# Reordering one stretch of a fused attention and highway kernel: batch 2's query exps and sums around batch 1's x

## The chip, the core and the metric

The kernel runs on one core of one Trainium2 chip. A core has five engines with queues of their own: TensorE (PE, matrix products), VectorE (DVE), ScalarE (ACT), GpSimd (POOL) and SyncE (SP, which here issues the transfers). PE writes its products into PSUM, which holds eight banks; the other operands lie in SBUF. The metric is the device time of a run in microseconds (us), as the median over several runs.

## The reference

Two layers follow each other. The first is a linear attention without a square score matrix: the queries are softmaxed over their 64 features, the keys over the 576 tokens, and a 64 by 64 product of keys and values is applied to the queries. The second is a highway layer over the joined heads.

```python
q_s = exp(q - max(q, -1));  q_s = q_s / (sum(q_s, -1) + 1e-09)
k_s = exp(k - max(k, 2));   k_s = k_s / (sum(k_s, 2) + 1e-09)
kv  = einsum('bhsd,bhse->bhde', k_s, v)
x   = einsum('bhsd,bhde->bhse', q_s, kv)      # then (4608, 512), heads side by side
H   = maximum(x @ w_h, 0)
T   = 1 / (1 + exp(-(x @ w_t + b_t)))
out = T * H + (1 - T) * x
```

There are 8 batches, 8 heads, 576 tokens and 64 features; inputs and output are 32-bit.

## The kernel before, in words

**Attention, one batch at a time.** `load` brings q, k and v of a batch (1152 KB each) into SBUF over SP's queue, in the order in which the loads are written. `exp_half` lets ACT take the exp of half the heads of q or k into a 16-bit tile (eq, ek). The query sums are either one DVE reduction per half (`q_sums`) or, for batches 1 and 2, a tree of two halving adds and a short reduction (`q_sums_tree`, L228 to L230); `q_recip` inverts them on DVE, and `q_scale_p` multiplies eq by them on POOL in pieces of tokens. `cast_v` and `cast_v_head` bring v to 16 bits, on POOL or ACT, with a column of ones behind every head, so that one product gives both the key-value product and the key sums. `q_trans` turns eq on PE (tile pq, three groups of tokens) and copies it to qsT on DVE. `kv_half` accumulates the key-value products of two heads' pairs in psk (two banks, called for half 0 and half 1), and `kv_norm` divides by the key sums on DVE (rz, kvn). `x_pair` multiplies qsT by kvn into two banks (px) for the first 512 tokens and copies each to the 16-bit tile xT, one on ACT and one on DVE; `x_left` does the last 64 tokens of all heads in two small products (px_l), copied by DVE to x9.

**Highway layer, one chunk at a time.** Chunk c is the first 512 tokens of batch c; chunks 8 and 9 gather all batches' last tokens. For each of four blocks of 128 output features, `gate` does four products into a bank pt, and ACT takes the tanh of it in place; `carry` does four products into a bank ph, and DVE makes relu(ph) minus x in one operation, the difference dd (L332); `blend` is a second DVE operation, (tanh + 1) times dd, into the 16-bit tile g (L340). `out_tile` turns x + g/2 back on PE (bank nat), copies it to 32 bits and stores it.

**PSUM.** Three pools share the eight banks: `ps_ht` has four (pt and ph), `ps_q` three (pq, psk, px, px_l) and `ps_nat` one. A new tile takes the bank that was freed first; PE waits until the last reader of that bank is done.

**Order.** Nothing is scheduled by a planner: the order of the Python calls is the order on every queue. First a list is run from top to bottom (the start, batches 0 and 1, chunk 0). After it come the entries of `events`, sorted by their place; chunk c lies at 8c to 8c + 7, with its gate of block ob at 8c + 2ob, its carry one later and its blend two later. The preparation of batch b is placed between the products of chunk b - 1, from the table with the places of its transposes (tr), key-value halves (kv) and x products (x). Within one place the order of insertion counts. Each engine works through its queue in that order, and an instruction that has to wait holds up all behind it on its engine.

Of the kernel before, what the change touches and what calls it, by code (L numbers as in the profile page):

```python
# [9 lines left out]
FP32 = mybir.dt.float32  # L10
# [8 lines left out]
def kernel(  # L19
# [10 lines left out]
    nc = tc.nc  # L30
    B, H, S, D = q.shape
    P = 128
    PAD = 128
    N9 = S // 64
    NM = N9 - 1
# [20 lines left out]
    ps_ht = pool("ps_ht", 4, space=PSUM)  # L56
    ps_q = pool("ps_q", 3, space=PSUM)
# [205 lines left out]
        else:  # L263
            nc.vector.tensor_copy(qsT[b][:, :, n0:n1, :], t[:, :, 0:w, :])  # L264

    def x_pair(b, a, even=False):
        g, b2 = b // 2, b % 2
        if a == 0 and b2 == 0:
            xT[g] = xtp.tile([P, 4, NM, 2, 64], FP16, tag="xT", name=f"xT_{g}")
        t = [  # L270
            ps_q.tile([P, NM, 64], FP32, tag="qx", name=f"px_{b}_{a}_{c}")
            for c in range(2)
        ]
        for x in range(2):
            for c in range(2):
                r = slice(64 * c, 64 * c + 64)
                mm(
                    t[c][64 * x : 64 * x + 64].rearrange("p n d -> p (n d)"),
                    kvn[b % 2][r, x, a, :],
                    qsT[b][r, 2 * a + x, 0:NM, :].rearrange("p n d -> p (n d)"),  # L280
                    True, True,
                )
        for c in range(2):
            dst = xT[g][:, 2 * a + c, :, b2, :]
            if (c == 0) if even else (a + c < 2):
                nc.scalar.copy(dst, t[c])  # L286
            else:
                nc.vector.tensor_copy(dst, t[c])  # L288
# [17 lines left out]
    def views(c):  # L306
        if c >= B:
            h = slice(4 * (c - B), 4 * (c - B) + 4)
            return lambda k_: x9[:, k_, h], lambda k_: g9[:, k_, h]
        g, b2 = c // 2, c % 2  # L310
        if g not in gT:
            gT[g] = gp.tile([P, 4, NM, 2, 64], FP16, tag="g", name=f"g_{g}")
        return lambda k_: xT[g][:, k_, :, b2, :], lambda k_: gT[g][:, k_, :, b2, :]

    live = {}
# [8 lines left out]
        live[c, ob] = ps  # L324

    def carry(c, ob):
        xv = views(c)[0]
        ps = ps_ht.tile([P, rows_of(c), 64], FP32, tag="ht", name=f"ph_{c}_{ob}")
        for k_ in range(4):
            mm(ps, w16["h"][:, k_, ob * P : ob * P + P], xv(k_), k_ == 0, k_ == 3)  # L330
        dd = mo.tile([P, rows_of(c), 64], FP16, tag="dd", name=f"dd_{c}_{ob}")
        nc.vector.scalar_tensor_tensor(  # L332
            dd, ps, 0.0, xv(ob), op0=ALU.max, op1=ALU.subtract
        )
        live[c, ob] = (live[c, ob], dd)
# [76 lines left out]
    def at(p, *fs):  # L412
        events.setdefault(p, []).extend(fs)

    E = lambda f, *a: (lambda: f(*a))

    for c in range(1, B + 2):
        for ob in range(4):
            p = 8 * c + 2 * ob
            at(p, E(gate, c, ob))  # L420
            at(p + 1, E(carry, c, ob))
# [14 lines left out]
    at(p + 4, E(tile9, 1, 4))  # L436
    at(p + 8, E(tile9, 2, 3), E(tile9, 3, 3), E(last9))

    at(8, E(exp_half, 2, "q", 1), E(cast_v, 2, 0))
    at(9, E(cast_v_head, 2, 2, nc.gpsimd))  # L440
    at(10, E(exp_half, 2, "k", 0), E(q_sums_tree, 2, 1), E(q_recip, 2))
    at(10, E(q_scale_p, 2, 0, 4), E(q_scale_p, 2, 4, 8), E(q_scale_p, 2, 8, N9))
    at(11, E(cast_v_head, 2, 3, nc.scalar), E(exp_half, 2, "k", 1))
    for b in range(2, B):
        p = 8 * (b - 1)
        if b > 2:
            s = p + {3: -2, 4: -4}.get(b, -5)
            at(s, E(exp_half, b, "q", 0))
            at(s + 1, E(exp_half, b, "q", 1), E(q_sums, b, 0))
            at(s + 2, E(q_sums, b, 1), E(q_recip, b))  # L450
            if b > 3:
                at(s + 2, E(q_scale_p, b, 0, 4))
                at(s + 3, E(q_scale_p, b, 4, N9))
            s = p + {3: 0, 4: 0}.get(b, -1)
            at(s, E(exp_half, b, "k", 0), E(cast_v, b, 0))
            at(s + 1, E(exp_half, b, "k", 1), E(cast_v, b, 1))
            if b == 3:
                at(p + 1, E(q_scale_p, b, 0, 4), E(q_scale_p, b, 4, N9))
        tr, kv, x = {
            2: ((5, 6, 6), (4, 5), (6.5, 7.5, 7.5)),  # L460
            3: ((4, 5, 5), (3, 4), (6, 7, 7)),
            4: ((2, 3, 4), (4, 5), (6, 6, 7)),
        }.get(b, ((2, 3, 4), (3, 4), (5, 6, 7)))
        for i in range(3):
            at(p + tr[i], E(q_trans, b, i))
        at(p + kv[0], E(kv_half, b, 0))
        at(p + kv[1], E(kv_half, b, 1), E(kv_norm, b))
        at(p + x[0], E(x_pair, b, 0))
        at(p + x[1], E(x_pair, b, 1))
        at(p + x[2], E(x_left, b))  # L470
# [3 lines left out]
    for f in [  # L474
        E(warm_up, 20),
        E(exp_half, 0, "q", 0), E(q_sums, 0, 0),
        E(exp_half, 0, "q", 1), E(q_sums, 0, 1),
        E(q_recip, 0), E(q_scale_v, 0, 0, 4), E(q_scale_v, 0, 4, N9),
        E(exp_half, 0, "k", 0), E(cast_v, 0, 0),
        E(exp_half, 0, "k", 1), E(cast_v, 0, 1),  # L480
        E(q_trans, 0, 0), E(q_trans, 0, 1), E(warm_up, 2), E(q_trans, 0, 2),
        E(warm_up, 6),
        E(kv_half, 0, 0), E(gate_bias), E(warm_up, 2), E(kv_half, 0, 1), E(kv_norm, 0),
        *[E(cast_weight, "t", k_, (nc.vector, nc.gpsimd)[k_ % 2]) for k_ in range(4)],
        E(warm_up, 4),
        E(x_pair, 0, 0), E(warm_up, 2), E(x_pair, 0, 1), E(warm_up, 1), E(x_left, 0),
        E(exp_half, 1, "q", 0), E(q_sums_tree, 1, 0),
        E(exp_half, 1, "q", 1), E(q_sums_tree, 1, 1), E(q_recip, 1),
        *[E(cast_weight, "h", k_, (nc.gpsimd, nc.scalar)[k_ % 2]) for k_ in range(4)],
        E(q_scale_p, 1, 0, 4), E(q_scale_p, 1, 4, 8),  # L490
        E(gate, 0, 0), E(gate, 0, 1), E(gate, 0, 2, (ps_q, "qx")), E(warm_mid, 5),
        E(carry, 0, 0), E(blend, 0, 0), E(carry, 0, 1), E(exp_half, 1, "k", 0),
        E(gate, 0, 3, (ps_nat, "nat")), E(blend, 0, 1), E(carry, 0, 2),
        E(q_trans, 1, 0), E(carry, 0, 3), E(blend, 0, 2),
        E(exp_half, 1, "k", 1),
        *[E(cast_v_head, 1, c, (nc.scalar, nc.gpsimd, nc.gpsimd, nc.scalar)[c]) for c in range(4)],
        E(q_scale_p, 1, 8, N9),
        *[E(load, 2, w) for w in "qk"], E(load, 2, "v", [nc.sync, nc.sync]),
        *[E(load, 3, w) for w in "qkv"],
        E(q_trans, 1, 1), E(kv_half, 1, 0), E(kv_half, 1, 1), E(kv_norm, 1),  # L500
        E(q_trans, 1, 2),
        E(x_pair, 1, 0, True), E(x_pair, 1, 1, True), E(exp_half, 2, "q", 0),
        E(blend, 0, 3), E(x_left, 1), E(q_sums_tree, 2, 0),
    ]:
        f()
    for p in sorted(events):
# [32 lines left out]
```

## Time and profile before

| what | value |
|---|---|
| median of 8 runs | 139.23 us (138.02 to 141.77) |
| the profiled execution | 139.1 us, its span 136.4 us |
| PE busy | 119.7 us, 88% of the span |
| DVE, ACT, POOL busy | 77%, 66%, 36% |
| transfers from 0 to some 50 us | about 410 GB/s, loads only |
| granted PE clock | 1.0 throughout |

The span is the time from the first to the last instruction that the profiler sees; 2.7 us of the profiled execution lie outside it. All times in the text are us from the span's start. A row of a queue gives start and length, the engine, the line, the operation, the tiles written and read, the number of instructions merged into the row, and in brackets how long the engine was idle before it and what ended that. A row of the chain gives start, length, engine, tile and line of what was waited for last. PE's rows overlap, since products are pipelined; all of them carry the line of a helper, L62 (`mm`) or, for transposes, L67, and are told apart by their tiles. L162 is `exp_half`, L235 `q_recip`, L247 `q_scale_p`. The stretch that the change touches begins at about 27 us and ends at about 47.

### The profile page before, as it was taken

Reading aid. Unit: us, or ns where it says so; the run is one execution under the profiler, and the core shown is the slowest. Engines: PE = TensorE matmul, PEld = TensorE weight load, DVE = VectorE, ACT = ScalarE, POOL = GpSimd, SP = SyncE. Lnnn points to the kernel's source line nnn. Section 1 sums busy time; section 2 is a strip of 40 time slices with the busy share of each in tenths; the row PEclk is TensorE's granted clock in tenths of the full one; section 3 lists DMA queues with packets and bytes.
Section 4 is the critical chain, followed back from the end, with each engine's and each line's share of the span. In section 5 each row is a group of like instructions: output and inputs, shape, how many; then the busy total and the mean of one; then the engine's idle time right before and its main releaser. Section 6 shows DMA issues by size and latency. Waiting matters only on the chain.

```text
span 136.4 us, 3607 instructions
## 1 busy us (share of the span) xinstructions
PE 119.7 (88%) x1499; PEld 68.7 (50%) x1499; DVE 105.0 (77%) x210; ACT 89.8 (66%) x132; POOL 49.6 (36%) x44
## 2 busy tenths in 40 slices
PE   4979997966968699969979999899899999999970
PEld 1335342543334256536644654475466456599950
DVE  1495638997978898996998789988988667588880
ACT  3660359926965698839978969778892654565640
POOL 2006305950575629049409800980395000000000
PEclk9999999999999999999999999999999999999999
DMA  4999999999999999964999899970033007046784
GB/s 159 347 390 400 411 391 411 411 413 406 411 407 407 412 412 416 400 263 195 318 400 406 276 302 405 392 322 0 2 149 166 5 0 308 0 185 271 296 329 154
DMA packets 15799, 40.06 MB, mean 294 GB/s; under 512 B 676, under 2 KB 1192, under 8 KB 14760
## 3 DMA queue, kind: packets, MB, share of 16 engines
q1 hardware_dynamic: 15784, 39.85, 75.4%
q8 instruction: 11, 0.18, 0.5%
q14 instruction: 4, 0.03, 0.1%
HBM read 30.41 MB, written 9.44 MB: 292 GB/s over the span
## 4 chain that ended last, share of the span: by engine, by line
PE 51%; DVE 22%; DMA 11%; ACT 5%; SPq 4%; POOL 2%; issue 2%; DVEq 0%; POOLq 0%
PE pt L62 16%; PE ph L62 15%; DMA w32h<-in_moe_w_h_dram 11%; PE nat L62 10%; DVE r L217 6%; DVE g L340 4%; DVE dd L332 4%; PE psk L62 4%; PE pq L67 4%; SPq L95 3%; ACT eq L162 2%; ACT xT L286 2%; DVE xT L288 2%; PE px L62 2%; POOL eq L247 1%
## 5 line engine op out<-in xcount | busy, mean ns | idle before, releaser
L247 POOL TENSOR_TENSOR eq<-eq,r 128x1024 f16<-128x1024 f16 (+2 forms) x16 | 29.7, 1874 | 29.8 <-DVE r L235 29.8
L323 ACT ACTIVATE pt<-pt,bt 128x512 f32<-128x512 f32 (+1 forms) x40 | 24.7, 621 | 22.4 <-PE pt L62 22.4
L62 PE MATMUL pt<-xT,w16t 128*128 128x512 f16 x128 | 33.3, 380 | 1.7 <-DVE xT L288 1.7
L62 PE MATMUL ph<-xT,w16h 128*128 128x512 f16 x128 | 33.0, 380 | 0.8 <-POOL w16h L114 0.8
L332 DVE SCALAR_TENSOR_TENSOR dd<-ph,xT 128x512 f16<-128x512 f32 x32 | 21.8, 682 | 8.0 <-PE ph L62 8.0
L340 DVE SCALAR_TENSOR_TENSOR g<-pt,dd 128x512 f16<-128x512 f32 (+1 forms) x40 | 25.2, 630 | 2.4
L162 ACT ACTIVATE eq<-q 128x1152 f16<-128x1152 f32 x16 | 18.5, 1168 | 3.9 <-DMA q<-in_q_dram 3.9
L174 POOL CAST v<-v 128x1152 f16<-128x1152 f32 x13 | 14.6, 1147 | 17.2 <-DMA v<-in_v_dram 17.2
L62 PEld LDWEIGHTS <-w16t 128*128 128x128 f16 x160 | 14.0, 98 | 12.3 <-issue 0.7
L62 PE MATMUL nat<-half_i,g 128*128 128x128 f16 x142 | 19.8, 219 | 0.1
L62 PEld LDWEIGHTS <-w16h 128*128 128x128 f16 x160 | 13.7, 98 | 12.2 <-POOL w16h L114 1.8
L162 ACT ACTIVATE ek<-k 128x1152 f16<-128x1152 f32 x16 | 18.5, 1167 | 1.4 <-DMA k<-in_k_dram 1.4
L286 ACT CAST xT<-px 128x512 f16<-128x512 f32 x23 | 12.9, 593 | 9.8 <-PE px L62 9.2
L217 DVE TENSOR_REDUCE r<-eq 128x18 f32<-128x1152 f16 x12 | 16.1, 1345 | 3.6 <-ACT eq L162 3.5
L371 ACT COPY o<-nat 128x512 f32<-128x512 f32 x28 | 16.6, 592 | 2.8 <-PE nat L62 2.0
L62 PE MATMUL nat<-ident,xT 128*128 128x128 f16 x128 | 17.7, 219 | 0.0
L264 DVE COPY qsT<-pq 128x1024 f16<-128x1024 f16 (+1 forms) x24 | 13.0, 553 | 3.7 <-PE pq L67 3.6
L62 PEld LDWEIGHTS <-g 128*128 128x128 f16 x144 | 14.0, 98 | 3.5 <-DVE g L340 0.6
L62 PEld LDWEIGHTS <-xT 128*128 128x128 f16 x128 | 12.5, 98 | 5.0 <-issue 2.6
L67 PE MATMUL pq<-ident,eq 128*128 128x128 f16 x144 | 11.8, 219 | 2.3 <-POOL eq L247 1.3
L62 PE MATMUL warm<-wide,ident 128*128 128x512 f16 x37 | 11.6, 461 | 1.9 <-DVE wide L143 1.9
L67 PEld LDWEIGHTS <-eq 128*128 128x128 f16 x144 | 9.0, 98 | 6.2 <-POOL eq L247 2.9
(49 smaller groups left out, 95.7 us busy)
## 6 DMA issues: line engine op xcount, KB each, us to landing
out_dram<-o SPq DMA_DIRECT2D x8, 1024.0 KB, 4.3
q<-in_q_dram SPq DMA_DIRECT2D x7, 1152.0 KB, 13.6
k<-in_k_dram SPq DMA_DIRECT2D x7, 1152.0 KB, 14.7
v<-in_v_dram SPq DMA_DIRECT2D x5, 1152.0 KB, 13.6
v<-in_v_dram SPq DMA_DIRECT2D x6, 576.0 KB, 12.0
q<-in_q_dram SPq DMA_DIRECT2D x2, 576.0 KB, 3.9
k<-in_k_dram SPq DMA_DIRECT2D x2, 576.0 KB, 6.6
w32t<-in_moe_w_t_dram SPq DMA_DIRECT2D x1, 1024.0 KB, 10.5
```

The source lines that it names most:

```text
L62: mm = lambda o, l, r, st, sp: nc.tensor.matmul(o, l, r, start=st, stop=sp, skip_group_check=True)
L67: nc.tensor.matmul(o, i, ident, is_transpose=True, start=True, stop=True, skip_group_check=True,)
L162: nc.scalar.activation(dst[b][:, :, 2 * a : 2 * a + 2, :], in32[which][b][:, 2 * a : 2 * a + 2].rearrange("p c n d -> p n c d"), AF.Exp,)
L174: (eng or nc.gpsimd).tensor_copy(o, i)
L217: nc.vector.reduce_sum(qsum[b][:, :, h], eq[b][:, :, h, :], axis=AX.X)
L247: nc.gpsimd.tensor_mul(e, e, r.broadcast_to(list(e.shape)))
L264: nc.vector.tensor_copy(qsT[b][:, :, n0:n1, :], t[:, :, 0:w, :])
L286: nc.scalar.copy(dst, t[c])
L323: nc.scalar.activation(ps, ps, AF.Tanh, bias=bt2[:, ob : ob + 1], scale=0.5)
L332: nc.vector.scalar_tensor_tensor(dd, ps, 0.0, xv(ob), op0=ALU.max, op1=ALU.subtract)
L340: nc.vector.scalar_tensor_tensor(gv(ob), th, 1.0, dd, op0=ALU.add, op1=ALU.mult)
L371: nc.scalar.copy(o, flat(t))
```

## The change

It touches the tail of the start list and the events from 8 to 16, that is batch 1's x, batch 2's preparation and chunk 1; all other calls stay as they are.

- `carry` is split into `carry_products` (PE) and `carry_diff` (DVE). For block 3 of chunk 0 the difference is run later, behind batch 1's last transposes, and blend(0, 2) comes ahead of the products; blend(0, 3) goes from ahead of x_left to place 10.5.
- Batch 2's first query exp stands ahead of batch 1's x products and copies, the second behind them, at the end of the list instead of at place 8. Both trees and the reciprocal close the list; the second tree and the reciprocal were at place 10.
- The second pair of batch 1's x is made in banks of `ps_ht` instead of `ps_q`.
- x_left of batch 1 goes from the list to place 8.2, behind the first gate of chunk 1.
- v of batch 2 is cast head by head: POOL, ACT, POOL, ACT. It was two heads at once on POOL, then one on POOL, one on ACT. The scale pieces of batch 2 go from place 10 to 8 (two) and 11 (one). The key exps go from 10 and 11 to 9 and 10.
- Batch 2's table: the third transposes at 6.4, the second key-value half at 6.2 (was 5), the x products at 7, 7.5 and 7.6.

```diff
-    def x_pair(b, a, even=False):
+    def x_pair(b, a, even=False, home=None):
+        ps, tag = home or (ps_q, "qx")
         t = [
-            ps_q.tile([P, NM, 64], FP32, tag="qx", name=f"px_{b}_{a}_{c}")
+            ps.tile([P, NM, 64], FP32, tag=tag, name=f"px_{b}_{a}_{c}")
             for c in range(2)
         ]
...
     def carry(c, ob):
+        carry_products(c, ob)
+        carry_diff(c, ob)
+
+    def carry_products(c, ob):
         xv = views(c)[0]
         ps = ps_ht.tile([P, rows_of(c), 64], FP32, tag="ht", name=f"ph_{c}_{ob}")
         for k_ in range(4):
             mm(ps, w16["h"][:, k_, ob * P : ob * P + P], xv(k_), k_ == 0, k_ == 3)
+        live[c, ob, "h"] = ps
+
+    def carry_diff(c, ob):
+        xv = views(c)[0]
+        ps = live.pop((c, ob, "h"))
         dd = mo.tile([P, rows_of(c), 64], FP16, tag="dd", name=f"dd_{c}_{ob}")
...
-    at(8, E(exp_half, 2, "q", 1), E(cast_v, 2, 0))
-    at(9, E(cast_v_head, 2, 2, nc.gpsimd))
-    at(10, E(exp_half, 2, "k", 0), E(q_sums_tree, 2, 1), E(q_recip, 2))
-    at(10, E(q_scale_p, 2, 0, 4), E(q_scale_p, 2, 4, 8), E(q_scale_p, 2, 8, N9))
-    at(11, E(cast_v_head, 2, 3, nc.scalar), E(exp_half, 2, "k", 1))
+    at(8, E(cast_v_head, 2, 0, nc.gpsimd), E(q_scale_p, 2, 0, 4), E(q_scale_p, 2, 4, 8))
+    at(8.2, E(x_left, 1))
+    at(9, E(exp_half, 2, "k", 0))
+    at(10, E(cast_v_head, 2, 1, nc.scalar), E(exp_half, 2, "k", 1))
+    at(10.5, E(blend, 0, 3))
+    at(11, E(cast_v_head, 2, 2, nc.gpsimd), E(cast_v_head, 2, 3, nc.scalar))
+    at(11, E(q_scale_p, 2, 8, N9))
...
-            2: ((5, 6, 6), (4, 5), (6.5, 7.5, 7.5)),
+            2: ((5, 6, 6.4), (4, 6.2), (7, 7.5, 7.6)),
...
-        E(q_trans, 1, 0), E(carry, 0, 3), E(blend, 0, 2),
+        E(q_trans, 1, 0), E(blend, 0, 2), E(carry_products, 0, 3),
...
-        E(q_trans, 1, 2),
-        E(x_pair, 1, 0, True), E(x_pair, 1, 1, True), E(exp_half, 2, "q", 0),
-        E(blend, 0, 3), E(x_left, 1), E(q_sums_tree, 2, 0),
+        E(q_trans, 1, 2), E(carry_diff, 0, 3), E(exp_half, 2, "q", 0),
+        E(x_pair, 1, 0, True), E(x_pair, 1, 1, True, (ps_ht, "ht")),
+        E(q_sums_tree, 2, 0), E(exp_half, 2, "q", 1), E(q_sums_tree, 2, 1), E(q_recip, 2),
```

## The prediction

> **What bounds the kernel now.** I read the busy shares first, then the chain of work that ended last, then a table by stage, then each engine's own queue from 20 to 62 us.
>
> ```profile
> PE 119.7 (88%) x1499; PEld 68.7 (50%) x1499; DVE 105.0 (77%) x210; ACT 89.8 (66%) x132; POOL 49.6 (36%) x44
> ...
> PE 51%; DVE 22%; DMA 11%; ACT 5%; SPq 4%; POOL 2%; issue 2%; DVEq 0%; POOLq 0%
> ```
>
> TensorE (PE) is the main engine, and the chain runs over it for half the span. But an average hides the stage that is edited. By stage (stretch, length, then busy time of each engine):
>
> ```profile
> 30.00:33.80 3.80, 2.29 (x21) 1.19 (x22) 3.08 (x11) 2.23 (x3) 0.00 (x0) 1.00 1.04 407
> 33.80:41.00 7.20, 5.80 (x89) 2.78 (x91) 5.99 (x14) 5.64 (x7) 4.52 (x4) 1.00 1.04 408
> 41.00:47.00 6.00, 4.16 (x71) 2.08 (x60) 4.73 (x11) 4.29 (x6) 3.86 (x4) 1.00 1.04 408
> 47.00:60.00 13.00, 12.56 (x165) 6.71 (x164) 12.26 (x23) 9.87 (x14) 4.37 (x3) 1.00 1.03 403
> ```
>
> From 30 to 47 us PE does 12.25 us of work in 17.0; from 47 on it is almost full (12.56 of 13.0). So 4.7 us of PE holes lie in the edited stretch, and what is won there before 47 us reaches the end only if nothing later waits for a transfer. The chain through the holes (start, length, what):
>
> ```profile
> 37.77 0.39 DVE r L235
> ...
> 38.30 1.91 POOL eq L247
> ...
> 40.25 0.62 PE pq L67 x8
> ...
> 42.88 1.15 ACT eq L162
> 44.03 1.01 ACT xT L286 x2
> 45.04 1.06 ACT eq L162
> 46.10 0.48 ACT xT L286
> ...
> 46.63 0.25 PE px_l L62 x4
> 46.88 1.04 PE pt L62 x4
> ```
>
> Batch 2's query sums end in a reciprocal at 37.77; GpSimd (POOL) can scale only then, and PE's transposes (pq) wait for it. Later the copies of batch 2's x share ScalarE (ACT) with batch 3's exps. The queues show three waits of PE:
>
> ```profile
> 28.98 0.79 PE L62 MATMUL psk<-v,ek 64*64 64x65 f16 x71 [0.86 <-DVE g L340]
> 40.25 0.62 PE L67 MATMUL pq<-ident,eq 128*128 128x128 f16 x8 [1.29 <-POOL eq L247]
> 46.63 0.25 PE L62 MATMUL px_l<-qsT,kvn 64*64 64x64 f16 x4 [1.29 <-ACT xT L286]
> ```
>
> **What the Trainium skill says.** "PSUM — Partial Sum Buffer", Engine vs sequencer instructions: ACT, VectorE (DVE) and POOL queues are strict first-in-first-out, and matmuls start in program order. The trace agrees: the x copy of 0.48 us at 46.10 runs only after the 1.06 us exp ahead of it. So an instruction's place counts as much as its inputs. The same page, Specifications: eight 2 KiB banks; the pools take 4+3+1, so a bank freed late stalls PE. "SBUF — State Buffer", Who interferes with whom: a DVE instruction with two SBUF inputs contends with a POOL instruction that reads SBUF. The trace agrees: the first halving add (L228) takes 0.53 us at 36.38 beside a POOL cast, 0.46 at 33.78 with POOL idle. "Perfetto Trace Analysis", Roofline: one core's transfers are bounded by its 16 DMA engines, about 435 GB/s; the trace's plateau is 407 to 413, so loads cannot land earlier.
>
> **The change, step by step.** Names are as in the code: blend(chunk, block) and so on. Back to back, DVE starts 512-column operations 0.60 apart (0.79 when a blend needs the difference just ahead); the three tree operations take 1.2, reciprocal ready 1.7 after the tree's start; ACT's exp occupies 1.1, its x copy 0.55, a v head 0.57, a tanh 0.6 (start-to-start distances from the queues). Four 512-column matmuls occupy PE 0.86, and the last is ready 1.04 after the first starts.
>
> 1. *blend(0, 2) ahead of the third difference.* Before, DVE ran carry(0, 3)'s difference at 27.65 and the blend at 28.25; batch 1's psk needs the bank that the blend frees, and resumed 0.73 after the blend's start. Now the blend starts at 27.65, psk at 28.38, the kvn result and px_1_0 at 29.78 instead of 30.38: gain 0.60. The difference itself moves to 30.12 on DVE; its bank is not asked for before that.
>
> 2. *Query exp of batch 2 ahead of batch 1's x copies on ACT.* The q transfer was issued at 16.38 and landed 13.6 later: 29.98. (Cross-check: v's first half released POOL at 34.5; 1.18 MB of k at 0.41 MB/us before it, and 0.59 MB of v, put q at 30.15.) Exp 30.0 to 31.2; the x copies, whose inputs are ready by 30.4, start at 31.1 and 31.65: cost 0.7. With px_1_1 in banks of the other pool it no longer waits for a copy, which before held it 0.51. DVE's two copies run 30.72 to 31.9. pt_1_0's third product waits for ACT's second copy, 32.25; with x_left after it, ph_1_0 starts at 32.9 instead of 33.79: gain so far 0.89.
>
> 3. *Both sums ahead of chunk 1's first difference on DVE.* Second exp on ACT 32.1 to 33.28. First tree 31.9 to 33.1, second 33.32, reciprocal ready 35.03, instead of 38.15; x_left's copies to 35.4. Behind them, and this is the price, dd_1_0 starts at 35.4 instead of 34.98. pt_1_2 needs dd_1_0's bank: 36.15 instead of 36.38, PE idle about 0.6 before it. Gain shrinks to 0.23. The trees have POOL idle beside them until 34.5.
>
> 4. *Scale on POOL.* v head 0 casts 34.5 to 35.12; scale 35.18 to 37.09 instead of 40.21, second piece to 38.94; the v head behind it to 39.6, last piece to 40.1. On ACT: tanh, key exp 33.8, tanh, v head 35.45 to 36.1, key exp to 37.15, v head to 37.75. psk_2 starts at 37.0, ph_1_2 at 37.4, pq_2_0 at 38.3 instead of 40.25: 1.95 gained. POOL is done 1.2 earlier, so what is late next is PE's own order.
>
> 5. *Order 6, 6.2, 6.4 on PE.* psk_2 now holds two banks of three while two pq's pass through the third. DVE: blend(1, 0) 36.19, blend(0, 3) 36.79, dd_1_1, blend(1, 1) 38.18, dd_1_2 38.78, qsT 39.38. So pq_2_1 starts at 40.1 (idle 0.5), psk_2's second half 40.55, and pq_2_2 after the second qsT at 41.5 (idle 0.5), ph_1_3 41.6, instead of 43.86.
>
> 6. *x of batch 2 after ph_1_3.* px_2_0 at 42.47 instead of 43.52. ACT copies 42.9 to 44.0, batch 3's second exp to 45.05, third copy to 45.55. DVE: dd_1_3 42.67, batch 3's first sum 43.28 to 44.54, copy to 45.2. px_l's second half waits for that copy, 45.25; pt_2_0 45.4, ph_2_0 46.26 instead of 47.75. **Gain 1.5.** Of the 2.26 at ph_1_3 this gives back 0.8, to ACT's exp and DVE's sum.
>
> 7. *Onwards.* PE has no hole from 47.75 to 54.6; the next long DVE stretch (54.63 to 60.84) starts at the end of a PE product, so it shifts whole. No later load is moved in SP's queue. Three loads wait for work here: q of batch 5 (issued 41.18) for the query exp's end, now 33.3; k (44.08) for the key exp, 37.15; v (46.86) for the casts, 39.6. All stay covered, as the queue is still pacing transfers then. If that cover failed, v's cast would slip by the lateness.
>
> Splitting carry into two functions, the two single heads in place of a two-head cast (0.67 twice against 1.15), and px in another pool's bank cost no work worth counting on a path: POOL sits idle for 5.4 us before 34.5.
>
> Sum: span 136.4 - 1.5 = 134.9. The profiled execution took 139.1, 2.7 more than its span, so 137.6; the median of the runs is 0.13 above it: **137.7**.
>
> **What is unmeasured.** The replay strings together some ten waits, each good to perhaps 0.1 us in either direction. q's landing is one record: 0.2 later takes 0.2 off. Steps 3 and 5 hold 1.6 us of predicted stalls on banks; at none of them the gain would be the 2.26 of ph_1_3 (137.0), at twice them nothing remains (139.3). Both ends go into the range; I take the replay.
>
> **Rivals.** *(a) DVE becomes the bound.* From 30 to 42 us it has hardly a gap in my replay; each bank PE wants is freed by an operation behind the sums. For: PE meets four such waits in steps 3, 5 and 6. Against: each was read from distances in this trace. If they run 1.0 worse in sum: 138.7, within 1%. *(b) The change reaches the end whole*, the exp of batch 3 hiding in the space won: 137.0. Against: ACT's second exp stands between the copies as before. *(c) Slower: ACT is blocked on q's transfer.* The exp now stands ahead of the x copies, so a late q holds ACT, these copies, pt_1_0 and all behind. Each us past 29.98 costs one; zero gain at 31.5, slower beyond; landing with k, near 33, gives 137.7 + 3.0 = 140.7. Against: q is the first in the queue after v of batch 1, and the transfers run at a steady 407 to 413 GB/s. *(d) The order isn't what the code says*: excluded, each engine's queue has the listed order; only how it waits is open.
>
> **Chances.** The forecast 0.50 (136.9 to 138.4), (a) 0.28, (b) 0.10, (c) 0.12. About 1%, 1.4 us, is what a measurement of this kernel can tell from no change; its eight runs spread over 2.7%. The forecast lies just past that line at -1.1%, so some 0.11 of its half falls within 1%. Faster: 0.39 + 0.10 = 0.49; within: 0.11 + 0.28 = 0.39; slower 0.12. Range 136.8 to 139.8: it holds the forecast, (a) and (b), and leaves out most of (c).
>
> **What would show it.** Right: the first query exp of batch 2 at 30.0 and ahead of the x copies; the reciprocal over near 35.0; POOL's scale starting near 35.2, with no wait of pq_2_0 for POOL; pt_1_2 near 36.15 after a short PE idle; ph_2_0 near 46.3. Wrong: a wait of ACT for q's transfer beyond 30.5; PE holes at pt_1_2, pq_2_1 or pq_2_2 well over 0.6; a stretch after 47 us longer than before.

## The result and the profile after

The changed kernel takes 137.12 us (median of 22 runs) against 139.41 for the kernel before beside it: a ratio of 0.9863, 95% interval 0.9836 to 0.9890, that is 1.9 us less (1.5 to 2.3). This ratio and all ratios below leave out the slow runs, those more than 1.5% above the fastest of their kernel, while the medians are over all runs and lie 2.3 us apart. Its profiled execution took 137.74 us, its span 134.9, where the kernel before had 139.1 and 136.4.

Two things differ between executions of the same code. The first transfers land earlier or later: batch 1's query exps, which need one of them, start between 17.89 and 20.29 us in the profiles of this document, though the instructions ahead of them are the same. And in some executions PE is granted half its clock for 3.41 us, which is called a drop below. So rows of two profiles are compared by their distance from a common event.

The page of the changed kernel, busy shares and the chain's shares by engine:

```profile
PE 119.3 (88%) x1499; PEld 68.4 (51%) x1499; DVE 104.8 (78%) x210; ACT 90.4 (67%) x133; POOL 49.1 (36%) x44
...
PE 53%; DVE 24%; DMA 13%; ACT 5%; issue 1%; SPq 0%; DVEq 0%
```

The work is the same; POOL has gone from the chain. The table by stage, in the same stretches as before (stretch, length, busy time of PE, PE's loads, DVE, ACT, POOL, then clock, share and rate of the transfers):

```profile
30.00:33.80 3.80, 2.77 (x24) 1.17 (x25) 3.68 (x9) 3.65 (x6) 0.00 (x0) 1.00 1.03 404
33.80:41.00 7.20, 6.67 (x110) 3.48 (x108) 6.79 (x15) 5.79 (x9) 5.56 (x5) 1.00 1.05 411
41.00:47.00 6.00, 4.19 (x38) 1.79 (x31) 5.43 (x13) 3.70 (x6) 2.23 (x2) 1.00 1.03 406
```

PE does 13.63 us of work from 30 to 47 us, where it did 12.25: 1.4 us of holes are filled. DVE is the engine without holes now: 10.47 of the 11.0 us from 30 to 41. The chain through the stretch (start, length, what):

```profile
16.45 13.68 DMA q<-in_q_dram
...
30.15 1.16 ACT eq L162
31.31 0.96 ACT xT L287 x2
32.27 1.07 ACT eq L162
...
33.37 0.47 DVE t L228
...
34.70 0.38 DVE r L235
...
36.11 1.29 DVE g L350 x2
...
40.05 0.62 PE pq L67 x8
```

It starts with the transfer of q of batch 2, runs over ACT (exp, x copies, exp) into DVE's tree and reciprocal, and through DVE's queue back to PE. The scale on POOL, on the chain before, is off it. The rows of the queues that answer to those shown before:

```profile
28.59 0.79 PE L62 MATMUL psk<-v,ek 64*64 64x65 f16 x71 [0.27 <-DVE g L350]
31.84 1.08 PE L62 MATMUL pt<-xT,w16t 128*128 128x512 f16 x4 [1.03 <-ACT xT L287]
38.30 0.61 PE L67 MATMUL pq<-ident,eq 128*128 128x128 f16 x8
45.21 0.25 PE L62 MATMUL px_l<-qsT,kvn 64*64 64x64 f16 x4 [0.88 <-DVE xT L289]
30.15 1.16 ACT L162 ACTIVATE eq<-q 128x1152 f16<-128x1152 f32 x1 [1.69 <-DMA q<-in_q_dram]
35.23 3.76 POOL L247 TENSOR_TENSOR eq<-eq,r 128x1024 f16<-128x1024 f16 x2
```

psk waits 0.27 for the blend's bank instead of 0.86. The transposes of batch 2 come at 38.30 with no wait for POOL (40.25, after a wait of 1.29). A new wait has come: pt_1_0 waits 1.03 for ACT's x copies, which now stand behind the exp, and ACT itself waits for q.

### The profile page after: what moved, and what is told of

It reads as the page before. It is cut to its first block, busy times and chain, and to the rows that moved or that the text cites. A ratio compares the mean times of both kernels' runs of the same rounds, so it can differ in the third digit from the quotient of the medians.

```text
span 134.9 us, 3608 instructions
## 1 busy us (share of the span) xinstructions
PE 119.3 (88%) x1499; PEld 68.4 (51%) x1499; DVE 104.8 (78%) x210; ACT 90.4 (67%) x133; POOL 49.1 (36%) x44
## 4 chain that ended last, share of the span: by engine, by line
PE 53%; DVE 24%; DMA 13%; ACT 5%; issue 1%; SPq 0%; DVEq 0%
PE pt L62 15%; PE ph L62 15%; DMA q<-in_q_dram 13%; PE nat L62 10%; DVE r L217 8%; PE pq L67 5%; DVE dd L342 4%; PE psk L62 4%; DVE g L350 3%; ACT eq L162 3%; PE warm L62 2%; DVE xT L289 2%; DVE qsT L264 2%; ACT xT L287 1%; DVE r L235 1%; DVE eq L243 1%
## 5 line engine op out<-in xcount | busy, mean ns | idle before, releaser
L174 POOL CAST v<-v 128x1152 f16<-128x1152 f32 x12 | 13.5, 1146 | 14.3 <-DMA v<-in_v_dram 14.3
```

Of the source, the lines that this page charges most:

```text
L174: (eng or nc.gpsimd).tensor_copy(o, i)
```

## The experiments

The first four ran on one chip (before: 139.68), the next four on another (139.10), the last three on a third (140.0 and 139.67). All ratios are against the kernel before on the same chip.

The span without a drop is the median span of the executions whose mean clock was 0.99 or more, with their number: 3.41 us at half clock take the mean of a span of 137 us down by 0.0125, so these had no drop while PE worked (the low clock behind the last product, which most profiles show, costs nothing). It says more of an order of instructions than the ratio, which also counts how many executions had drops; but of two or four executions it is rough. For the kernel before it is 136.6 beside the first four, 136.5 beside the next four, and 136.5 and 137.0 in the two sets of the third chip.

The other columns are from the profile: px_1_0's start, the start of batch 2's first query exp ("exp"), and the distance from px_1_0 to the start of batch 2's first transposes and of two products that close chunk 1 and open chunk 2. From px_1_0 on, a later start upstream drops out of the distances; the landing of q doesn't, as its transfer doesn't wait for px_1_0. Where the exp waits for q, the distance from the exp says more. A star marks a profile, or a distance, with a drop on the way.

| kernel | ratio to before (95%) | span without a drop | px_1_0 | exp | pq_2_0 | ph_1_3 | ph_2_0 |
|---|---|---|---|---|---|---|---|
| before | 1 | 136.6 (27 of 67) | 30.38 | 32.58 | 9.87 | 13.48 | 17.37 |
| changed | 0.9863 (0.9836 to 0.9890) | 134.8 (14 of 23) | 29.99 | 30.15 | 8.31 | 11.55 | 16.27 |
| e1_px_one_pool * | 0.9959 (0.9922 to 0.9997) | 136.15 (4 of 22) | 29.70 | 30.20 | 9.96 | 13.20 | 17.92 |
| e2_diff_first | 0.9876 (0.9845 to 0.9908) | 135.0 (13 of 22) | 30.31 | 30.21 | 8.05 | 11.29 | 16.01 |
| e3_exp_after_copies | 0.9927 (0.9895 to 0.9958) | 135.2 (12 of 22) | 29.46 | 31.06 | 8.93 | 12.18 | 17.05 * |
| e4_sum_late | 0.9998 (0.9947 to 1.0049) | 136.2 (4 of 14) | 29.32 | 29.81 | 9.75 | 13.12 | 18.72 * |
| e5_old_table | 0.9892 (0.9838 to 0.9947) | 135.4 (2 of 6) | 30.40 | 30.57 | 8.32 | 12.75 | 16.65 |
| e6_after_q_late * | 1.0150 (1.0096 to 1.0204) | none of 6 | 29.25 | 32.61 | 12.81 | 15.85 | 20.57 |
| e7_before_q_late * | 1.0053 (1.0015 to 1.0090) | 136.65 (8 of 22) | 30.05 | 32.62 | 10.83 | 14.43 | 18.33 |
| e8_batch3_behind | 0.9888 (0.9827 to 0.9948) | 134.75 (2 of 6) | 29.80 | 30.13 | 8.47 | 11.72 | 14.93 |
| e9_batch3_sum_up | 0.9837 (0.9773 to 0.9901) | 134.7 (4 of 6) | 30.56 | 30.80 | 8.38 | 11.63 | 14.84 |
| e10_after_again * | 0.9886 (0.9826 to 0.9946) | 135.25 (4 of 6) | 31.08 | 31.32 | 9.48 | 12.53 | 17.24 |
| e11_q_in_halves | 0.9838 (0.9775 to 0.9902) | 134.85 (4 of 6) | 29.47 | 28.53 | 8.17 | 11.41 | 16.13 |

**Both pairs of x in one pool (e1).** Only the home of the second pair is undone.

```diff
-        E(x_pair, 1, 0, True), E(x_pair, 1, 1, True, (ps_ht, "ht")),
+        E(x_pair, 1, 0, True), E(x_pair, 1, 1, True),
```

> The changed kernel, but with the second pair of batch 1's x back in the three banks of ps_q. My theory (the second product of that pair must again wait for ACT's first x copy, which ends at 31.8 behind the query exp; DVE's second copy, the first tree and so both sums and chunk 1's first difference move with it): DVE's first tree starts near 32.8 instead of 32.04, the reciprocal ends near 35.8 instead of 35.08, pt_1_2 near 36.8 instead of 36.06; the time is 0.7 us above the changed kernel's 137.1: 137.8. Rival (the other pool's banks matter for nothing, the sums wait for the exps anyway): 137.1.

Measured: 139.18 us, ratio 0.9959, some 1.3 us above the changed kernel's ratio, and 1.35 by the spans without a drop. The queues of PE, DVE, ACT and POOL:

```profile
31.89 0.64 PE L62 MATMUL px<-qsT,kvn 64*64 64x512 f16 x3 [1.41 <-ACT xT L287]
32.59 0.69 DVE L289 CAST xT<-px 128x512 f16<-128x512 f32 x1 [1.35 <-PE px L62]
33.04 1.17 ACT L162 ACTIVATE eq<-q 128x1152 f16<-128x1152 f32 x1
34.40 0.45 DVE L228 TENSOR_TENSOR t<-eq 128x576 f16<-128x576 f16 x1
34.88 0.65 DVE L229 TENSOR_TENSOR t<-t 128x288 f16<-128x288 f16 x1
34.66 0.71 POOL L182 CAST v<-v 128x576 f16<-128x576 f32 x1 [6.03 <-PE px_l L62]
```

The wait is there, as the theory has it, but the cost is about twice what it gave. The second pair has to wait for an ACT copy that stands behind the exp; DVE's own second copy waits 1.35 for that pair, and both trees stand behind this copy in DVE's queue. ACT's second exp is late too (33.04), but it doesn't set the pace: it is over at 34.21, and the second tree starts only at 34.40, when the first is done. Counted from q's exp, the reciprocal ends 6.23 behind it instead of 4.93, and ph_1_3 comes 1.31 later. Of the 1.30, 0.23 is a drop from 31.66 to 35.07: the three products take 0.64 instead of 0.41. That leaves 1.07, where the theory gave 0.7. It left out that the second tree now runs beside POOL's v cast, where its second add takes 0.65 instead of 0.31.

**The third difference first (e2).** Step 1 alone is undone.

```diff
-        E(q_trans, 1, 0), E(blend, 0, 2), E(carry_products, 0, 3),
+        E(q_trans, 1, 0), E(carry, 0, 3), E(blend, 0, 2),
...
-        E(q_trans, 1, 2), E(carry_diff, 0, 3), E(exp_half, 2, "q", 0),
+        E(q_trans, 1, 2), E(exp_half, 2, "q", 0),
```

> The changed kernel, but with chunk 0's third difference ahead of blend(0, 2), as before. Step 1 of the prediction counted 0.6 us of gain here; then the time is 0.6 above the changed kernel's 137.1: 137.7. Rival, from the profile after (ACT is held by the query exp until 31.22, so an x product that is ready at 30.6 or at 31.2 starts its copy at the same time): psk and px_1_0 come 0.3 to 0.6 later, but pt_1_0 starts within 0.1 of 31.84; the time is 137.1 to 137.3.

Measured: 137.56 us, ratio 0.9876, not to be told from the changed kernel's 0.9863. The queue of PE:

```profile
28.91 0.79 PE L62 MATMUL psk<-v,ek 64*64 64x65 f16 x71 [0.85 <-DVE g L350]
31.90 1.08 PE L62 MATMUL pt<-xT,w16t 128*128 128x512 f16 x4 [0.77 <-ACT xT L287]
```

psk waits the full 0.85 again, 0.58 more than in the changed kernel, and px_1_0 comes 0.32 later; yet pt_1_0 starts only 0.06 later, as it waits 0.26 less for ACT, and by 0.06 the exp is later too. From the exp on the two profiles are equal: pq_2_0 8.15, ph_1_3 11.39, ph_2_0 16.11 after it in both. The interval alone would still allow the 0.6 of the theory; the rows don't, and the spans without a drop differ by 0.2. The rival is right: ACT, held by the exp till 31.3, hides step 1.

**The query exp behind the x copies (e3).**

```diff
-        E(q_trans, 1, 2), E(carry_diff, 0, 3), E(exp_half, 2, "q", 0),
-        E(x_pair, 1, 0, True), E(x_pair, 1, 1, True, (ps_ht, "ht")),
+        E(q_trans, 1, 2), E(carry_diff, 0, 3),
+        E(x_pair, 1, 0, True), E(x_pair, 1, 1, True, (ps_ht, "ht")), E(exp_half, 2, "q", 0),
```

> The changed kernel, but with batch 2's first query exp behind batch 1's x copies on ACT instead of ahead of them. Theory (the DVE chain from the second sum to the banks is what counts, and the exps feed it): pt_1_0 starts about 0.6 earlier (31.2), yet the second exp ends near 33.9 instead of 33.34, the reciprocal near 35.7 instead of 35.08, pt_1_2 and POOL's scale follow by the same 0.6: 137.7. Rival (the exp ahead of the copies is a cost, 0.7 in step 2 of the prediction, which undoing gives back): 136.5.

Measured: 138.25 us, ratio 0.9927, some 0.9 us above the changed kernel by the ratio, 0.4 by the spans without a drop. PE and DVE:

```profile
36.16 1.02 PE L62 MATMUL pt<-xT,w16t 128*128 128x512 f16 x4 [1.25 <-DVE dd L342]
32.27 0.46 DVE L228 TENSOR_TENSOR t<-eq 128x576 f16<-128x576 f16 x1 [0.68 <-ACT eq L162]
```

The x copies do start earlier and ph_1_0 comes 2.68 after px_1_0 instead of 3.05. But the exp is late for the tree, DVE stands still for 0.68, and PE gives the lead back at pt_1_2, 1.25 of waiting for a bank. From px_1_0 to ph_1_3 0.63 is lost. But px_1_0 was early in this profile: q's transfer was issued at 16.39 and took 13.5, so it had landed at 29.9, 0.4 behind px_1_0, and the changed kernel would have had to wait for it. Counted from that landing ph_1_3 comes 11.75 behind, where the changed kernel has 11.39, so some 0.35 is lost; the reciprocal ends at 35.17, not at the 35.7 that was expected. The sign is the theory's, and the second exp and the sums behind it are what counts. The size is some 0.4; the 0.9 of the ratios is uncertain by 0.6 either way.

**The second sum late (e4).** Second tree, reciprocal and two scale pieces go back to place 10.

```diff
-    at(8, E(cast_v_head, 2, 0, nc.gpsimd), E(q_scale_p, 2, 0, 4), E(q_scale_p, 2, 4, 8))
+    at(8, E(cast_v_head, 2, 0, nc.gpsimd))
...
+    at(10, E(q_sums_tree, 2, 1), E(q_recip, 2), E(q_scale_p, 2, 0, 4), E(q_scale_p, 2, 4, 8))
...
-        E(q_sums_tree, 2, 0), E(exp_half, 2, "q", 1), E(q_sums_tree, 2, 1), E(q_recip, 2),
+        E(q_sums_tree, 2, 0), E(exp_half, 2, "q", 1),
```

> The changed kernel, but with the second tree, the reciprocal and the first two scale pieces back at place 10, behind chunk 1's first blend. Theory (the early reciprocal is what frees POOL and with it pq_2_0): pt_1_2 comes 0.4 earlier (near 35.65), the reciprocal ends near 37.2 instead of 35.08, pq_2_0 starts near 39.25 instead of 38.30 and waits for POOL, and 1.0 us of the gain is lost: 138.1. Rival (the sums ahead of the difference only hold up the banks, the loss of step 3): the time is at or below the changed kernel's, 136.6 to 137.1.

Measured: 139.70 us, ratio 0.9998: by the ratio the whole gain is gone, more than the 1.0 that the theory gave. PE and POOL:

```profile
39.07 0.62 PE L67 MATMUL pq<-ident,eq 128*128 128x128 f16 x8 [1.37 <-POOL eq L247]
40.93 0.62 PE L67 MATMUL pq<-ident,eq 128*128 128x128 f16 x8 [0.37 <-POOL eq L247]
37.12 3.76 POOL L247 TENSOR_TENSOR eq<-eq,r 128x1024 f16<-128x1024 f16 x2 [1.70 <-ACT ek L162]
```

The wait for POOL is back at 1.37 (before: 1.29), and a second one behind it. POOL had been done with its cast for 1.70 when the reciprocal came; what it waited for is the reciprocal over at 36.97, though the row names an ACT exp. At ph_1_3 1.57 of the changed kernel's 1.93 is lost; counted from q's exp, which came 0.33 later against px_1_0 here, 1.24. The spans without a drop say the same: 136.2 is 1.4 above the changed kernel's 134.8, with 136.6 before, so 1.4 of 1.8 is lost. The rest of the 1.9 lies within the interval of 0.5% either way, and more of e4's executions had a drop: 10 of 14, against 9 of 23 in the changed kernel.

**Batch 2's old places (e5).**

```diff
-            2: ((5, 6, 6.4), (4, 6.2), (7, 7.5, 7.6)),
+            2: ((5, 6, 6), (4, 5), (6.5, 7.5, 7.5)),
```

> The changed kernel, but with batch 2's old table of places on PE: the second key-value half ahead of the fourth gate, x products at 6.5, 7.5 and 7.5. Theory: the second key-value half waits for the v head that POOL casts behind two scale pieces (ready 39.6), the fourth gate then starts near 40.05 instead of 38.75, but the x products come ahead of ph_1_3 again; ph_2_0 starts about 0.3 later than 46.26: 137.4. Rival (the new places are worth as much as the sums, about 1 us): 138.1.

Measured: 137.40 us, ratio 0.9892, 0.4 us above the changed kernel: what the theory gives, and inside the noise of both. PE:

```profile
40.14 0.48 PE L62 MATMUL psk<-v,ek 64*64 64x65 f16 x36 [0.81 <-POOL v L182]
45.92 0.25 PE L62 MATMUL px_l<-qsT,kvn 64*64 64x64 f16 x4 [1.29 <-ACT xT L287]
```

The second key-value half now waits for a v head that POOL casts behind the scale. ph_1_3 comes 1.20 later, but at ph_2_0 only 0.38 of that is left: the old places have batch 2's first x products ahead of ph_1_3, and these come no later here (12.41 after px_1_0, 12.51 in the changed kernel). The rival's 1.0 lies within the interval; ph_2_0 speaks against it.

**q of batch 2 late, in the changed kernel (e6) and in the kernel before (e7).** The same edit in both:

```diff
-        *[E(load, 2, w) for w in "qk"], E(load, 2, "v", [nc.sync, nc.sync]),
+        *[E(load, 2, w) for w in "kq"], E(load, 2, "v", [nc.sync, nc.sync]),
```

> The changed kernel, but batch 2's k is loaded ahead of its q, so that q lands near 33.0 instead of 30.13 with the same bytes. Theory (rival (c) of the prediction: ACT is blocked on q with the x copies behind it): the first query exp starts near 33.0, the x copies near 34.1 instead of 31.22, pt_1_0 near 34.7 instead of 31.84, and 2.8 us are lost: 139.9. Rival (later slack takes most of it up): under 138.5.

> The kernel before, with the same exchange of the loads of k and q of batch 2. Theory (there the exp stands behind the x copies and started at 32.58, so q has 2.6 us to spare): the exp starts near 33.0, the time is within 0.5 us of the kernel before, 139.4 to 139.9. Rival (q's landing bounds that kernel too): 141 or more.

Measured: e6 140.96 us, ratio 1.0150, some 4.0 us above the changed kernel; e7 140.30 us, ratio 1.0053 (1.0015 to 1.0090), 0.7 us. PE and ACT in e6:

```profile
34.29 1.87 PE L62 MATMUL pt<-xT,w16t 128*128 128x512 f16 x4 [4.22 <-ACT xT L287]
32.61 1.16 ACT L162 ACTIVATE eq<-q 128x1152 f16<-128x1152 f32 x1 [4.67 <-DMA q<-in_q_dram]
```

and ACT in e7:

```profile
30.70 0.59 ACT L286 CAST xT<-px 128x512 f16<-128x512 f32 x1 [2.72 <-PE px L62]
32.62 1.16 ACT L162 ACTIVATE eq<-q 128x1152 f16<-128x1152 f32 x1 [0.26 <-DMA q<-in_q_dram]
```

q lands at the same 32.6 in both. In e7 the x copies are done by then, ACT waits 0.26, and the exp is where it was before (32.58). In e6 everything behind the exp stands: PE 4.22. So it is the change that makes the kernel depend on q's landing, and rival (c) of the prediction is a real mechanism that did not strike. e7 itself lost a little more than the 0.5 that was expected. Without a drop five of its eight spans are 136.6 or 136.7, beside a median of 136.5 before, but three are 137.8 to 139.3, where none of the kernel before on that chip was above 136.9; whether q's landing makes these three long isn't shown. The exp of e6 is 2.46 later than in the changed kernel, though px_1_0 was 0.74 earlier. Of the rest of the 4.0 us 1.1 lies between the exp and ph_1_3 (12.49 instead of 11.39), where a drop of 6.83 us begins within the wait. All six runs of e6 had a mean clock of 0.982 or less, that is a drop; so what the late q costs without one, 2.8 by the expectation, isn't shown.

**Batch 3's second exp and first sum behind batch 2's x (e8).** An attempt to win back what step 6 gives away, on top of the changed kernel.

```diff
-            at(s + 1, E(exp_half, b, "q", 1), E(q_sums, b, 0))
+            if b == 3:
+                at(15.55, E(exp_half, b, "q", 1))
+                at(s + 2, E(q_sums, b, 0))
+            else:
+                at(s + 1, E(exp_half, b, "q", 1), E(q_sums, b, 0))
...
-        at(p + x[0], E(x_pair, b, 0))
-        at(p + x[1], E(x_pair, b, 1))
+        at(p + x[0], E(x_pair, b, 0, b == 2))
+        at(p + x[1], E(x_pair, b, 1, b == 2, (ps_ht, "ht") if b == 2 else None))
```

> The changed kernel, with the same treatment for batch 2's x: its second pair in banks of ps_ht, one copy of each pair on ACT and one on DVE, and batch 3's second query exp and first query sum behind those copies and the blend. Theory (the PE waits of 0.47 and 0.88 at 43.59 and 45.21 are ACT's exp and DVE's sum ahead of the copies): ph_2_0 starts near 44.8 instead of 46.26, but the reciprocal of batch 3 ends near 48.4 instead of 48.06 and PE then waits for it at pt_2_2 and pq_3_0, so 0.6 to 0.7 us remain: 136.5. Rival (PE is full afterwards, all 1.5 us remain): 135.6. Second rival (batch 3's sums set the pace, nothing remains): 137.1.

Measured: 137.05 us, ratio 0.9888 (0.9827 to 0.9948): nothing that can be told from the changed kernel. PE and DVE:

```profile
44.73 1.02 PE L62 MATMUL ph<-xT,w16h 128*128 128x512 f16 x4
48.99 1.02 PE L62 MATMUL pt<-xT,w16t 128*128 128x512 f16 x4 [0.65 <-DVE dd L342]
59.08 0.38 PE L62 MATMUL pt<-xT,w16t 128*128 128x512 f16 x1 [0.85 <-DVE xT L289]
45.38 2.60 DVE L217 TENSOR_REDUCE r<-eq 128x18 f32<-128x1152 f16 x2
```

ph_2_0 comes at 44.73, 1.53 earlier than in the changed kernel, as worked out. Of this 0.27 is left at the last product of pt_3_0 (59.35 there). The second rival is right that nothing remains: DVE's sums of batch 3, now in one piece of 2.60, end no earlier (48.39 with the reciprocal, 48.06 there), and PE stands 0.65 at a bank that DVE frees behind them.

**Batch 3's first sum up again (e9), beside the changed kernel (e10).** e9 is e8 with that sum ahead of blend(1, 3) and x_left of batch 2 behind two products of chunk 2.

```diff
-                at(s + 2, E(q_sums, b, 0))
+                at(15.7, E(q_sums, b, 0))
...
-        at(p + x[2], E(x_left, b))
+        at(17.2 if b == 2 else p + x[2], E(x_left, b))
```

> The kernel before this one in the series (batch 3's sums behind the blend) won 1.5 us at ph_2_0 and kept 0.27 of it, because batch 3's reciprocal stayed at 48.4. Here batch 3's first sum stands ahead of blend(1, 3) and batch 2's last tokens go behind two products of chunk 2. Theory (batch 3's sums, and the scale behind them, set the pace from 48 us on): the first sum starts near 44.4, the reciprocal ends near 47.9, 0.5 earlier, and the time is 0.5 to 0.7 below that of the changed kernel, near 136.5. Rival (DVE's total work from 42 to 60 us is the bound, in whatever order): no measurable difference from the changed kernel, 137.1.

> The changed kernel itself once more, on the same chip and against the same runs of before as the version beside it: 137.1, ratio 0.986. It is there so that the two can be compared directly, and to see how far two profiled executions of one kernel differ at the same rows (ph_2_0 at 46.26 in the first; 0.3 either way expected).

Measured: e9 136.94 us, ratio 0.9837 (0.9773 to 0.9901); e10 137.45 us, ratio 0.9886 (0.9826 to 0.9946). The reciprocal ends 18.11 after px_1_0 in e9 and 18.59 in e8, the 0.48 that the theory gives; but the changed kernel has 18.07, so these sums are not all that sets the pace. The last product of pt_3_0 starts 28.86 after px_1_0, in e8 29.28, in the changed kernel 29.36. So e9 is ahead by 0.5 in the trace and by 0.51 in the medians, which agree; but the intervals overlap, and without a drop its span of 134.7 stands beside 135.25 in e10 and 134.8 in the first runs of the changed kernel. A better version is not shown. A stretch of the profile of e10 (columns as in the table by stage):

```profile
33.00:37.00 4.00, 3.99 (x18) 1.38 (x18) 3.48 (x11) 3.25 (x4) 1.21 (x2) 0.57 1.04 405
33.02:36.43 3.41, 3.41 (x16) 1.13 (x16) 3.11 (x10) 3.01 (x4) 0.64 (x2) 0.50 1.04 405
```

and PE's queue in it:

```profile
33.01 1.86 PE L62 MATMUL pt<-xT,w16t 128*128 128x512 f16 x4 [1.10 <-ACT xT L287]
35.06 1.70 PE L62 MATMUL ph<-xT,w16h 128*128 128x512 f16 x4
```

The same code as the first profile of the changed kernel reaches ph_2_0 at 48.32 instead of 46.26, well outside the 0.3 that I expected. 1.09 of that is there at px_1_0 (31.08): q of batch 1 landed so much later, its exps start at 20.29 instead of 19.20. The other 0.97 is the drop: half the clock from 33.02 to 36.43 us. Its span is 137.0, longer by the same 2.1.

**q of batch 2 in two transfers (e11).**

```diff
-        *[E(load, 2, w) for w in "qk"], E(load, 2, "v", [nc.sync, nc.sync]),
+        E(load, 2, "q", [nc.sync, nc.sync]), E(load, 2, "k"), E(load, 2, "v", [nc.sync, nc.sync]),
```

> Counted from the start of batch 2's first query exp, which is when q has landed, the changed kernel, the version with the third difference first and the version with batch 3's first sum up reach pq_2_0, ph_1_3 within 0.01 us of each other (8.15 and 11.39); so q's landing looks like the head of the chain. Here q of batch 2 is brought in two transfers of 576 KB, and at 0.41 MB/us the first half lands 1.4 us sooner, near 28.8. Theory (DVE is right behind q): the exp runs 28.8 to 29.9 and the x copies on ACT start near 30.5, 0.7 earlier; but DVE's own copies still run 30.85 to 32.04 and the trees behind them, so the reciprocal ends at most 0.2 earlier (34.9), and the time is 137.0, not to be told from the changed kernel. Rival (q's landing sets all that follows): reciprocal 0.7 earlier, 34.4, ph_2_0 at 45.5, 136.4.

Measured: 137.27 us, ratio 0.9838 (0.9775 to 0.9902), not to be told from the changed kernel. One of its six runs took 175.14 us, at a mean clock of 0.66; nothing on record says why. ACT, DVE and POOL:

```profile
28.53 1.16 ACT L162 ACTIVATE eq<-q 128x1152 f16<-128x1152 f32 x1 [0.36 <-DMA q<-in_q_dram]
30.12 1.07 ACT L287 CAST xT<-px 128x512 f16<-128x512 f32 x2 [0.42 <-PE px L62]
30.33 1.28 DVE L289 CAST xT<-px 128x512 f16<-128x512 f32 x2
34.04 0.38 DVE L235 RECIPROCAL r<-r 128x36 f32<-128x36 f32 x1
34.61 0.66 POOL L182 CAST v<-v 128x576 f16<-128x576 f32 x1 [6.24 <-DMA v<-in_v_dram]
```

The exp is 1.6 earlier and no copy waits for it. But DVE copies x 0.86 after px_1_0's start, as in the changed kernel, and its trees come behind: the reciprocal ends 4.95 after px_1_0 instead of 5.09, and ph_2_0 comes 0.14 sooner. The theory is right: DVE's queue is as late as q, within 0.14, and the chain that the profile showed is one of two that are nearly tied. The tie isn't fixed: in e8 the exp starts 0.33 after px_1_0 instead of 0.16, and there q is some 0.3 behind DVE's queue. POOL would not have profited either, since its v cast still ends at 35.2.

The losses of e1, e3 and e4 add up to more than the whole gain (1.35, 0.4 and 1.4 of 1.8 without a drop). The parts of the change need each other, so a loss by undoing one is not that part's share of the gain.

## Why the prediction was right

Forecast 137.7, measured 137.12; predicted span 134.9, measured 134.9. The rows of the stretch show that the replay was right, and this is no luck: they came, one after the other, where it put them. It is luck that q's landing, on which they hang, came within 0.15 of the one record that the replay took (in e10 it was 1.2 later still), and that the span agrees to the last digit: the 14 executions of the changed kernel without a drop range from 134.2 to 135.3, and e10, the same code, had 137.0.

- **Step 1** (0.60 gained at psk): the mechanism is right, the wait of 0.86 became 0.27, and 0.85 again in e2. But the gain is worth nothing at the end. By step 2's own times ACT is at the exp until 31.1, so nothing that px_1_0 wins can pass it; the prediction wrote down a gain that the next step swallowed.
- **Step 2** (exp ahead of the x copies, "cost 0.7"): times within 0.2 (exp 30.15, copies from 31.22, ph_1_0 33.04 for 32.9). Taken alone it is no price. e3 saves this cost and is 0.4 to 0.9 us slower: PE only comes sooner to the bank that DVE frees, while the sums come later. The prediction booked the cost here and what it buys in step 3.
- **The bank in the other pool**, which step 2 gave as 0.51 of waiting gone, was undersized: taking it back costs 1.3 us in e1, because DVE's second copy waits for that pair and both trees stand behind it, and the second tree then shares its time with a cast on POOL.
- **Steps 3 and 4** (reciprocal ready 35.03, scale 35.18, pq_2_0 38.3): 35.08, 35.23, 38.30. e4 shows that the gain hangs on them. The price, dd_1_0 at 35.4 and pt_1_2 at 36.15, came as worked out (35.33, 36.06), the idle ahead of pt_1_2 shorter in the record (0.26 for 0.6).
- **Step 5** (ph_1_3 at 41.6): 41.54; the two idles of 0.5 are recorded as 0.27 and 0.37. The new table by itself is worth 0.4 us or nothing (e5).
- **Step 6** (0.8 of 2.26 given back): 2.32 at ph_1_3 (43.86 to 41.54) and 1.49 at ph_2_0, so 0.83. e8 shows that it can't simply be taken back.
- **Step 7** (the rest shifts whole): the last store is issued at 131.64, before at 133.13, again 1.49; no load came late.
- **Rivals.** (a) DVE did become a bound of the stretch, level with q's landing, as e11 shows, but its delays were already in the replay, so no 1.0 was to be added. (b) The measured 137.12 is nearer to its 137.0 than to the forecast, but its mechanism did not happen: 0.83 of the 2.32 was given back, as step 6 has it. (c) did not strike, since q landed at 30.13 for 29.98; e6 and e7 show that the mechanism is right and that the change brings it. For q at 32.6 its rule of one us for each gives 140.3, and 140.96 was measured, with a drop in every run.

What was off is the term that turns the span into the median. The sum adds 2.7 us outside the span and 0.13 to the median. But 2.7 belongs to that one profiled execution: the median over the runs of the changed kernel, and over the 115 runs of the kernel before beside the experiments, is 2.0. And the profile before had no drop, while 65 of those 115 runs had one or more; their median span is 137.5, where the profile has 136.4. The two slips nearly cancel before (136.4 + 2.7 and 137.5 + 2.0) and don't after: 9 of 23 runs of the changed kernel had a drop, its median span is 135.1, and with 2.0 that is the measured 137.1. Whether the change itself makes drops rarer isn't shown. Without a drop the span went from 136.5 or 136.6 to 134.8, by 1.7 to 1.8; of the difference from the predicted 1.5, some 0.15 is that q of batch 2, the head of the chain, landed that much later in the changed profile than in the one before.

## What to carry to other kernels

Replay each engine's queue from the start-to-start distances of one trace, with each instruction that waits holding those behind it: here this gave more than ten times within about 0.2 us, while the worth of one edit by itself, read from one wait, was off by a factor of about two (e1) or had the wrong sign (e3). Ask of every gain whether the next engine is held by something else until later anyway (e2). Compare times only between executions of like clock, and add to a span the usual time outside it, not that of one execution. Work that feeds a long path (sums, reciprocal, scale, transposes) may go ahead of work whose delay the next bank wait absorbs anyway. When a chain begins at a transfer, see how far behind the next engine is before you move the transfer (e11: 0.14 us), and note that an instruction put ahead on such a transfer has made it critical (e6).

## What the runs showed of the hardware

- PE's granted clock drops in single executions, e10 beside the first profile of the same code. In the clock records of e1, e3, e4, e7 and e10 it is 0.50 for 3.41 us, in e6 for 6.83, twice as long; ahead and behind it is 1.00. In e10 the four products of a bank took 1.86 us instead of 1.08, while DVE's halving adds in the same stretch kept their length (0.31). Each drop began 23.9, 27.3 or 41.0 us after the first entry of its clock record, that is 7, 8 or 12 times 3.41.
- Cut into stretches of 3.41 us from that first entry on, PE was busy for 1.77 us (e1) to 2.01 us (e4) in the stretch ahead of each drop. No stretch with more than 2.05 us was followed by one, but four with 1.58 to 1.99 (two in e4, one each in e3 and e7) weren't either. So a wait matters by how it falls on these stretches, which lie differently in each execution; that PE's idle time brings a drop on fits this, and isn't shown.
- The landing of an early transfer scatters: batch 1's exps start at 19.20 and 20.29 in two executions of the changed kernel, and px_1_0 follows by the whole 1.09. An earlier landing isn't passed on whole: in e4 they start at 17.89, 1.31 earlier, and px_1_0 comes 0.67 earlier.
- A halving add on DVE with both operands in SBUF took 0.31 us with POOL idle (the changed kernel) and 0.65 beside a cast on POOL that had begun 0.22 us before it (e1).
